# Holding two weight loads behind the stores of a pair's finer sums in a planned MoE kernel

## The chip, the cores and the metric

The kernel runs on one core of one Trainium2 chip. The metric is the device time of one execution in microseconds, as the median of the runs shown. One further execution was recorded by the hardware profiler; every view of the profile quoted here comes from such an execution. TensorE is called PE, its weight load PEld, VectorE DVE, ScalarE ACT, GpSimd POOL. SP is the engine whose queue carries most DMAs.

## The reference

A linear attention over 8 batches and 8 heads (576 tokens, head size 64) gives x with 4608 rows and 512 columns. Then comes a mixture of 8 experts in which every row goes through every expert:

```python
logits = x @ w_gate
P = np.exp(logits - logits.max())
for _ in range(8):                      # the routing
    P /= P.sum(1, keepdims=True) + 1e-09
    P /= P.sum(0, keepdims=True) + 1e-09
    P *= N / E
for e in range(E):
    h = np.maximum(x @ w1[e], 0.0)      # up:   512 -> 1024
    out += P[:, e:e + 1] * (h @ w2[e])  # down: 1024 -> 512
```

## The kernel before

**Stages.** The attention of all batches takes the first 203 us of the profiled execution. In its gaps, expert 0 already runs for the groups of 512 rows whose x is complete (`up0`, L1005, and `down0`, L1010). Next, expert 0's remaining groups fill PE while DVE does the eight rounds of the routing (`routing`, L1146). In each round DVE makes column sums `cs` (L1170, split into three bf16 parts at L1179), one small PE matmul adds them over the partitions (`ps<-cs,colw` in the views, recorded under the helper's line L622), and DVE goes on from its result (L1185 to L1167 of the next round). Then experts 1 to 7 follow, about 107 us each. They use sums and differences of blocks (a fast matrix multiplication with seven products in place of eight), so the inputs x, the weights w1 and w2 and the hidden rows all need preparing subtractions on DVE (`sub`, L1236, whose instruction is recorded as L1240).

**The sums of x.** For each pair of row groups, `sums_x` (L1428) makes three combinations in buffers of the ring X and stores them to DRAM (L1422). For experts 2 to 7, three of the blocks get a second, finer level: `fine_x` (L1365) stores two parts of the block itself (L1369, L1371), makes four finer differences in one more buffer of X, and stores that buffer (L1385) to a DRAM tile Xi, one for each pair and block. The blocks are named "11", "21" and "t1", in this order. The ring X has four buffers (L492). Three are held by the pair's own sums while expert 1 works on that pair, so the three finer sums of a pair share the fourth: the subtractions of the next block wait until the store of the one before has landed. Pair 0's sums are made at 203 us, beside the routing; the other pairs' sums are made during expert 1. From expert 2 on, `load_fine` (L1389) reads everything back.

**The weights.** `load_w` (L514) loads both matrices of one expert, 2 MB of float32 in DRAM each, which become bf16 on the way, by two DMAs from POOL (L517). w1 and w2 have two buffers each, one of them a view of a tile `wx` that the attention uses before (tile `w` is the other). `sums_up` (L1242) and `sums_down` (L1291) prepare them; the second writes its results into `hx`. From expert 1 on, POOL's other work is the additions into acc (L1875) and some of M (L1643).

**What sets the order.** Nothing is written to an engine directly. Every operation is registered in a plan (`Plan.op`) with keys that it reads (r) and writes (w), and a duration. `Plan.schedule` (L271) then plays the whole program through and always starts the operation with the earliest possible time, ties by registration (L302). What results is one fixed list. `Plan.run` (L337) goes through that list and emits the instructions, so that each engine gets its own in that order and runs them strictly in that order; the waits between engines are made by the framework from the tiles that an instruction really reads and writes. The keys themselves are no waits on the chip. Only one rule is carried over as a wait of its own, for operations of DVE and POOL at a port that they share (`behind`).

**How the plan reckons DMAs.** `dma` (L428) gives every transfer a time on a link: bytes over a speed (L425; 540 bytes per ns for the sums' stores, 400 for the weights, L433). `Links` (L127) has one line for POOL's transfers and one for all others, each in order. A transfer joins its line 3.1 us after the issue on POOL and 1.6 us after it elsewhere (L136); it lands 1.0 us after its link time (L307). While both lines are busy, each is slowed:

```python
share = [1.0, 1.0]
if len(on) == 2:
    a, b = (x[0][2] for x in self.line)
    all_ = (0.61 if a.turn else 0.84) / (a.unit + b.unit)
    share = [all_ * a.unit, all_ * b.unit]
```

A store of the sums has unit 50, a weight matrix 150, so a store then goes at 0.84 * 50 / 200 = 0.21 of its speed and the load at 0.63.

**The loop over experts**, around the change (L1978 on): for each expert `load_w` is registered first; for expert 1 with the key "late" (the attention's buffers are free), for later ones also with a key of acc that expert e-1 writes, which places the loads late in that expert. Then expert 1 registers `sums_x` of pair 0; `sums_up`, `sums_down` and the loop over the pairs follow.

Of the kernel before, what the change touches and what calls it, by code (L numbers as in the profile page):

```python
# [349 lines left out]
def kernel(  # L350
# [44 lines left out]
    acc = [accp.tile([128, 4, DD], FP32, name=f"acc{g}", tag=f"acc{g}") for g in range(NA)]  # L395
# [12 lines left out]
    late = {}  # L408
# [19 lines left out]
    def dma(queue, nbytes, rate, fn, r=(), w=()):  # L428

        speed, unit = LINK.get(rate, (rate, 40))  # L430
        if nbytes == 2 << 20:
            speed, unit = 400, 150
        o = plan.op(queue, 0.8 if queue == "POOL" else 0.6, 0.0, fn, r, w, (), nbytes / speed)  # L433
        o.turn, o.unit = rate == 148, unit
# [71 lines left out]
    def new(tag):  # L506
        return R[tag].new()
# [3 lines left out]
        return buf().bitcast(BF16)  # L511


    def load_w(e, r=()):  # L514
        w1, w2 = new("w1"), new("w2")
        for w, src in ((w1, moe_w1), (w2, moe_w2)):
            dma("POOL", 2 << 20, 280, lambda w=w, src=src: nc.gpsimd.dma_start(  # L517
                out=w(), in_=src[e].rearrange("(c p) f -> p c f", p=128)),
                r, [(w, i, j) for i in range(2) for j in range(2)])
        return w1, w2  # L520
# [510 lines left out]
    for b in range(2):  # L1031
# [4 lines left out]
        w=["wphi_f0"])  # L1036
    dma("ACT", 1 << 15, 100, lambda: nc.scalar.dma_start(out=wphi_f[64:128, :], in_=w_phi),
        w=["wphi_f1"])
# [13 lines left out]
    for i in range(2):  # L1052
        dve(450, lambda i=i: nc.vector.memset(vrd[i], 0.0),
            w=[("vrd", i, h, *y) for h in range(2) for y in ((), (1,))])
# [181 lines left out]
    def sub(eng, el, out_, x, y, op, r, w):  # L1236
        f = nc.vector if eng is dve else nc.gpsimd
        kw = {"shared": True} if eng is dve else {}
        eng(el * 0.5 if eng is dve else el * 1.04 + 128,
            lambda: f.tensor_tensor(out=out_(), in0=x(), in1=y(), op=op), r, w, **kw)  # L1240

    def sums_up(e, w1):  # L1242

        def q(i, j):
            return lambda: w1()[:, 2 * j:2 * j + 2, 512 * i:512 * i + 512]

        S = [None] + [new("T") for _ in range(3)]

        def s(n):
            return lambda: S[n]().rearrange("p (a b) -> p a b", a=2)  # L1250


        a11, a12, a21, a22 = (1, 0), (1, 1), (0, 0), (0, 1)
        late = ["late"] + (["P"] if e == 1 else [])

        def k(a):
            return [(w1, *a)]

        sub(dve, 1024, s(2), q(*a11), q(*a21), ALU.subtract, k(a11) + k(a21) + late, [S[2]])
        sub(dve, 1024, q(*a21), q(*a21), q(*a22), ALU.add, k(a22) + late, k(a21))  # L1260
        sub(dve, 1024, s(1), q(*a21), q(*a11), ALU.subtract, k(a21) + k(a11) + late, [S[1]])
        sub(dve, 1024, s(3), q(*a12), s(1), ALU.subtract, k(a12) + [S[1]] + late, [S[3]])
        A = {"11": (q(*a11), k(a11)), "12": (q(*a12), k(a12)), "22": (q(*a22), k(a22)),
             "s1": (q(*a21), k(a21)), "s2": (s(1), [S[1]]), "s3": (s(2), [S[2]]),
             "s4": (s(3), [S[3]])}
        if e > 1:
            for n in INNER:
                fine_up(A, n)
        return A

    def fine_up(A, n):

        f, r = A[n]
        t, key, first = FINE_W[n]

        def a(q, k):
            return lambda: f()[:, k, :].rearrange("p (f q c) -> p q f c", f=2, q=2)[:, q]

        def s(n):
            return lambda: t()[:, n]  # L1280

        def step(n, x, y, op, r, w):
            sub(dve, 256, s(n), x, y, op, r, [(key, n), *w])

        step(0, a(1, 0), a(1, 1), ALU.add, r, first)
        step(2, a(0, 0), a(1, 0), ALU.subtract, r, [])
        step(1, s(0), a(0, 0), ALU.subtract, [*r, (key, 0)], [])
        step(3, a(0, 1), s(1), ALU.subtract, [*r, (key, 1)], [])
        A[n + "*"] = t, [(key, i) for i in range(4)]
# [28 lines left out]
    def xq(gs, i, j):  # L1318

        n = len(gs)  # L1320
        return lambda: xT[:, 2 * i:2 * i + 2, 512 * gs[0]:512 * (gs[0] + n)].rearrange(
            "p k (a b) -> p a k b", a=n)[:, :, :, 256 * j:256 * j + 256]

    def xall(gs):
        return [k for g in gs for k in xkeys(g)]
# [12 lines left out]
    class Turns:  # L1338
# [4 lines left out]
        def next(self):  # L1343
# [16 lines left out]
    Xi = {(g[0], n): dram.tile([128, 7, 256], BF16, name=f"xi{g[0]}{n}")  # L1360
          for g in pairs for n in INNER.values()}
# [54 lines left out]
    def new_x():  # L1416
        return {n: new("X") for n in (2, 3, 4)}

    def move_x(gs, n, store, X):
        d, t = (lambda: Xd[gs[0], n][:, 0:len(gs)]), (lambda: X[n]()[:, 0:len(gs)])  # L1420
        if store:
            dma("SP", len(gs) << 17, 160, lambda: nc.sync.dma_start(out=d(), in_=t()),  # L1422
                [X[n]], [("Xd", gs[0], n)])
        else:
            dma("SP", len(gs) << 17, 160, lambda: nc.sync.dma_start(out=t(), in_=d()),
                [("Xd", gs[0], n)], [X[n], "order of X"])

    def sums_x(gs, r0=()):  # L1428

        X = new_x()  # L1430

        def x(n):
            return lambda: X[n]()[:, 0:len(gs)]

        b11, b12, b21, b22 = (xq(gs, *ij) for ij in ((0, 1), (0, 0), (1, 1), (1, 0)))
        el, keys = 512 * len(gs), xall(gs)
        r = keys + ["late", *r0]
        sub(dve, el, x(3), b22, b12, ALU.subtract, r, [X[3], "order of X"])
        sub(dve, el, b12, b12, b11, ALU.subtract, ["late", *r0], keys)
        sub(dve, el, x(2), b22, b12, ALU.subtract, r, [X[2]])  # L1440
        sub(dve, el, x(4), b21, x(2), ALU.subtract, r + [X[2]], [X[4], "order of X"])
        for n in (3, 2, 4):
            move_x(gs, n, True, X)
        if len(gs) == 2:
            for n, b in (("22", b22), ("11", b11), ("21", b21), ("t1", b12)):
                if n in INNER.values():
                    fine_x(gs, n, b, r0)
                else:
                    for a in range(2):
                        dma("SP", 1 << 17, 160, lambda n=n, a=a, b=b: nc.sync.dma_start(  # L1450
                            out=Xp[gs[0], n][:, a], in_=b()[:, a]), r, [("Xp", gs[0], n, a)])
        return X
# [507 lines left out]
    def take():  # L1960
        z = [new(f"H{n}") for n in sorted(slots[:2])]
        del slots[:2]
        return z
# [13 lines left out]

    early, dn = [plain(8)], plain(7)  # L1978
    for e in range(1, E):
        w1, w2 = load_w(e, ["late", ("acc", 4, 0, 0)] if e > 1 else ["late"])  # L1980
        if e == 1:
            nextX = sums_x(pairs[0])
        A7 = sums_up(e, w1)
        B7 = sums_down(e, w2) if e > 1 else None
        turn = [*pairs, (8,)] if e < E - 1 else [(8,), *pairs]
        if e == 2:
            o = plan.op("X", 0.0, 0.0, lambda: None, w=["K"])
            for d in plan.ops[:-1]:
                if any(b.ring is R["X"] for b in d.bufs):
                    d.users.append(o)  # L1990
                    o.deps.append(d)
                    o.left += 1
        for n, gs in enumerate(turn):
            if (e, n) == (1, 4):
                plan.inorder = 1
            X = nextX if e == 1 else load_fine(gs)
            H = {g: [] for g in gs}
            for fp in range(len(gs)):
                hs = take()
                for i, z in enumerate(hs):  # L2000
                    H[gs[min(i, len(gs) - 1)]].append(z)
                fine = e > 1 and len(gs) == 2
                if fine:
                    un = up49(A7, fp, X, H, gs, ["up0", "K"])
                else:
                    un = up7(A7, gs, fp, X, H, ["up0"])
                for o in UNITS[turns.pop(0)]:
                    if o in un:
                        un[o]()
                    elif len(o) == 3:  # L2010
                        un[o[:2], int(o[2])]()
                    elif dn is not None:
                        dn[o]()
                if dn is not None:
                    dn["out"]()
                    slots.extend(dn["slots"])
                if e == 1 and fp == 0 and n + 1 < len(turn):
                    nextX = sums_x(turn[n + 1], [(H[gs[0]][0], 0, 1, 1)])
                if B7 is None and fp:
                    B7 = sums_down(e, w2)  # L2020
                if fp == len(gs) - 1:
                    wait += [(e, g, H[g], B7, w2, [z.ring.number for z in H[g]]) for g in gs]
                dn = next_down()
# [35 lines left out]
```

## Time and profile before

| what | value |
|---|---|
| median of 3 runs | 1010.11 us (1009.81 to 1011.59) |
| profiled execution, its time | 1010.62 us |
| its span from first to last instruction | 1008.8 us |
| PE, DVE, ACT, POOL busy | 994.0, 898.6, 812.8, 447.6 us |
| both loads of expert 1 issued at | 203.4 and 204.2 us |
| both loads of expert 2 issued at | 316.0 and 316.8 us |

How to read the views: times are microseconds from the start of the span. A row of the order of time gives start, duration, engine, line, operation, written tile <- read tiles, the count of merged instructions, and in brackets the engine's idle time before it with what ended it. A row of the waits gives who waited for whom, the total, the number of times, and the longest. A row of the chain of work gives start, length and what the end of the program then depended on. SPq is SP's queue, and its rows are issues of DMAs; "DMA to landing" is the time from an issue until its data have arrived. PE's matmul rows overlap in time (each is pipelined behind the one before), so their starts tell the rate. A row of the table by stretches gives the stretch, its length, and then the busy time of PE, PEld, DVE, ACT and POOL with counts.

### The profile page before, as it was taken

The page shows a single profiled execution, that of the slowest core. Times are in us where ns is not written, and L with a number is a line of the kernel's source. Part 1 is how long each engine was busy: PE and PEld are TensorE (multiplying, and loading weights), DVE is VectorE, ACT ScalarE, POOL GpSimd, SP SyncE. Part 2 cuts the span into 40 slices and gives each one's busy share as a digit, 9 for nine tenths or more (in the row PEclk, how much of TensorE's full clock was granted, in tenths as well). Part 3 has the DMA queues.
Part 4 walks back from the last instruction along what each step waited for, and adds up shares of the span by engine and source line. Part 5 has one row for each costly group of instructions (what it writes and reads, how often), then busy time and mean ns, then how long its engine had stood idle before and what let it go on. Part 6 is the DMA issues. An engine that isn't in the chain of part 4 may idle for free.

```text
span 1008.8 us, 23309 instructions
## 1 busy us (share of the span) xinstructions
PE 994.0 (99%) x8376; PEld 727.7 (72%) x8376; DVE 898.6 (89%) x1999; ACT 812.8 (81%) x1930; POOL 447.6 (44%) x514
## 2 busy tenths in 40 slices
PE   7899999999999999999999999999999999999998
PEld 5666666644566877777777877787778777787775
DVE  7999998987888998899989898989889988989886
ACT  7999999845979788878878788777887888778874
POOL 5778674400133344434444444444443444344443
PEclk9999999999999999999999999999999999999999
DMA  9999999181136423282327133632246222724653
GB/s 249 183 202 183 157 153 144 38 170 56 53 121 143 147 97 98 84 184 96 109 98 170 44 100 131 130 127 98 97 117 177 97 98 84 147 79 142 208 174 126
DMA packets 129748, 128.86 MB, mean 128 GB/s; under 512 B 55776, under 2 KB 98272, under 8 KB 129632
## 3 DMA queue, kind: packets, MB, share of 16 engines
q1 hardware_dynamic: 97680, 103.33, 36.3%
q0 software_dynamic: 31648, 23.86, 16.9%
q8 instruction: 65, 1.06, 0.5%
q14 instruction: 51, 0.42, 0.2%
q10 hardware_dynamic: 304, 0.20, 0.1%
HBM read 122.50 MB, written 19.53 MB: 141 GB/s over the span
## 4 chain that ended last, share of the span: by engine, by line
PE 92%; DVE 3%; ACT 2%; DMA 2%; issue 1%; POOL 0%; DVEq 0%
PE ps L1466 41%; PE ps L1475 20%; PE ps L622 17%; PE ps L1607 11%; PE ps L905 2%; DMA xi6t<-X 1%; DMA xi<-X 1%; PE ps L752 1%; ACT q L618 0%; DVE m L614 0%; ACT k L618 0%; DVE wx L614 0%; DVE X L1240 0%; DMA acc<-in_k_dram 0%; DVE hs L1676 0%
## 5 line engine op out<-in xcount | busy, mean ns | idle before, releaser
L1875 POOL TENSOR_TENSOR acc<-acc,hx 128x512 f32<-128x512 f32 x186 | 236.1, 1276 | 404.7 <-ACT hx L1872 135.0
L1466 PEld LDWEIGHTS <-hs 128*128 128x128 bf16 x1984 | 194.1, 98 | 46.4 <-issue 0.2
L1872 ACT ACTIVATE hx<-ps,P 128x256 f32<-128x256 f32 x372 | 158.9, 483 | 53.4 <-PE ps L1466 52.0
L1860 DVE SCALAR_TENSOR_TENSOR acc<-ps,P,acc 128x256 f32<-128x256 f32 x372 | 162.2, 478 | 30.2 <-PE ps L1466 28.2
L1475 PE MATMUL ps<-xT,T 128*128 128x512 bf16 x608 | 171.0, 379 | 0.0
L1466 PEld LDWEIGHTS <-hx 128*128 128x128 bf16 x1488 | 145.6, 98 | 24.9
L1466 PE MATMUL ps<-hx,hs 128*128 128x256 bf16 x992 | 144.3, 273 | 0.0
L1676 DVE CUSTOM_DVE_ANT_0 hs<-ps,U 128x512 bf16<-128x512 f32 x192 | 124.7, 684 | 11.3 <-PE ps L1475 6.6
L1607 PE MATMUL ps<-xT 128*128 128x256 bf16 x576 | 125.4, 272 | 0.0
L1475 PEld LDWEIGHTS <-T 128*128 128x128 bf16 x672 | 65.8, 98 | 40.6
L1682 ACT ACTIVATE hs<-ps 128x512 bf16<-128x512 f32 x96 | 55.9, 598 | 41.7 <-PE ps L1475 40.2
L1466 PE MATMUL ps<-wx,hs 128*128 128x256 bf16 x560 | 78.4, 273 | 0.0
L622 PE MATMUL ps<-w,hx 128*128 128x512 bf16 x288 | 73.0, 379 | 0.0
L622 PE MATMUL ps<-xT,w 128*128 128x512 bf16 x288 | 72.9, 379 | 0.0
L1466 PE MATMUL ps<-wx,hx 128*128 128x256 bf16 x496 | 72.3, 273 | 0.0
L1676 DVE CUSTOM_DVE_ANT_0 hs<-ps,X 128x512 bf16<-128x512 f32 x96 | 65.1, 684 | 7.8 <-PE ps L1607 6.9
L1466 PE MATMUL ps<-hx 128*128 128x256 bf16 x496 | 71.2, 273 | 0.0
L1607 PEld LDWEIGHTS <-xT 128*128 128x128 bf16 x576 | 56.3, 98 | 17.5
L1466 PE MATMUL ps<-w,hx 128*128 128x256 bf16 x432 | 62.2, 273 | 0.0
L614 DVE TENSOR_REDUCE m<-ps 128x4 f32<-128x512 f32 x88 | 58.8, 680 | 3.7 <-PE ps L622 1.9
L1672 ACT COPY X<-ps 128x512 f32<-128x512 f32 x96 | 58.6, 610 | 2.5 <-DVE ps L1650 2.5
L1466 PE MATMUL ps<-w,hs 128*128 128x256 bf16 x432 | 60.2, 273 | 0.0
(174 smaller groups left out, 2256.0 us busy)
## 6 DMA issues: line engine op xcount, KB each, us to landing
xT<-xi SPq DMA_DIRECT2D x48, 448.0 KB, 4.6
xT<-xd SPq DMA_DIRECT2D x72, 256.0 KB, 4.0
wx<-in_moe_w_dram POOLq DMA_DIRECT2D x8, 1024.0 KB, 11.2
v_m<-in_v_dram SPq DMA_DIRECT2D x15, 512.0 KB, 5.2
out_dram<-acc SPq DMA_DIRECT2D x14, 512.0 KB, 3.0
w<-in_moe_w_dram POOLq DMA_DIRECT2D x6, 1024.0 KB, 11.0
xT<-xp SPq DMA_DIRECT2D x24, 256.0 KB, 2.8
qk<-in_k_dram POOLq DMA_DIRECT2D x12, 256.0 KB, 5.4
```

The costliest lines, as they stand in the source:

```text
L614: dve(el, lambda: nc.vector.tensor_reduce(out=dst(), in_=src(), axis=AX.X, op=ALU.max, apply_absolute_value=True), r, w)
L622: nc.tensor.matmul(out_, lhsT=lhsT, rhs=rhs, start=start, stop=stop)
L905: pe(65, lambda j=j: nc.tensor.matmul(pn()[:, j * D1:j * D1 + D1], lhsT=s["T"][x]()[:, j % 2, 2 * h + j // 2, :] if j < 4 else r["T"][x]() ...
L1466: pe(256, lambda i=i, k=k, z=z: nc.tensor.matmul(bank()[:, 256 * i:256 * i + 256], lhsT=lhs(k, i), rhs=rhs(k), start=first and z, stop=k = ...
L1475: pe(512, lambda k=k: nc.tensor.matmul(bank().rearrange("p (a b) -> p a b", a=2), lhsT=lhs(k), rhs=rhs(k), start=first and k == 0, stop=k ...
L1607: pe(256, lambda: nc.tensor.matmul(halves_of(bank[q], n)(), lhsT=lhs(), rhs=t()[:, rhs, :], start=start, stop=True, skip_group_check=True) ...
L1672: act(512, lambda: nc.scalar.copy(out=flat(to[q])(), in_=bank[q]()), [bank[q]], [(to[q], 0), (to[q], 1)])
L1676: dve(515, lambda: nc.vector._custom_dve(ADD_SAT, out=out_(q, i, j), in0=bank[q]().rearrange("p (a b) -> p a b", a=2), in1=to[q](), s0=3.0 ...
L1682: act(512, lambda: nc.scalar.activation(out=out_(q, i, j), in_=bank[q]().rearrange("p (a b) -> p a b", a=2), func=ACT.Relu, bias=0.0, scal ...
L1860: dve(320, lambda n=n, ts=ts: nc.vector.scalar_tensor_tensor(out=acc[g][:, ts, 256 * j:256 * j + 256], in0=bank()[:, 256 * n:256 * n + 256 ...
L1872: act(370, lambda n=n: nc.scalar.activation(out=u()[:, n, :], in_=bank()[:, 256 * n:256 * n + 256], func=ACT.Copy, bias=0.0, scale=P[:, 4 ...
L1875: pool(695, lambda: nc.gpsimd.tensor_tensor(out=acc[g][:, 2 * i:2 * i + 2, 256 * j:256 * j + 256], in0=acc[g][:, 2 * i:2 * i + 2, 256 * j: ...
```

## The change

`load_w` takes one set of keys for w1 (`r`) and another for w2 (`r2`). For experts 1 and 2, w2's set gets one more key: the last store (part 2, the finer differences) of block "t1" of pair 0 for expert 1, and of pair 6 (row groups 6 and 7) for expert 2. The key must exist when the load is registered, so expert 1's `sums_x` of pair 0 is registered ahead of its loads. Experts 3 to 7 keep their keys.

```diff
-    def load_w(e, r=()):
+    def load_w(e, r, r2):
         w1, w2 = new("w1"), new("w2")
-        for w, src in ((w1, moe_w1), (w2, moe_w2)):
+        for w, src, r in ((w1, moe_w1, r), (w2, moe_w2, r2)):
             dma("POOL", 2 << 20, 280, lambda w=w, src=src: nc.gpsimd.dma_start(
                 out=w(), in_=src[e].rearrange("(c p) f -> p c f", p=128)),
                 r, [(w, i, j) for i in range(2) for j in range(2)])
...
     for e in range(1, E):
-        w1, w2 = load_w(e, ["late", ("acc", 4, 0, 0)] if e > 1 else ["late"])
         if e == 1:
             nextX = sums_x(pairs[0])
+        r = ["late", ("acc", 4, 0, 0)] if e > 1 else ["late"]
+        stored = [("Xi", 6 * (e - 1), "t1", 2)] if e < 3 else []
+        w1, w2 = load_w(e, r, r + stored)
         A7 = sums_up(e, w1)
```

## The prediction

> **What bounds the kernel now.** I read the page's span and busy shares first, then the chain of work that ended last, then the waits of PE, then the order of time on POOL, DVE and PE around the two loads that the diff touches.
>
> ```profile
> span 1008.8 us, 23309 instructions
> PE 994.0 (99%) x8376; PEld 727.7 (72%) x8376; DVE 898.6 (89%) x1999; ACT 812.8 (81%) x1930; POOL 447.6 (44%) x514
> PE 92%; DVE 3%; ACT 2%; DMA 2%; issue 1%; POOL 0%; DVEq 0%
> 336.00:960.00 624.00, 623.85 (x5007) 489.67 (x5006) 563.36 (x1212) 499.75 (x1215) 274.44 (x260) 1.00 0.41 116
> ```
>
> The reader is to see that TensorE is the limit: 994.0 of 1008.8 us busy, 92% of the chain. The last row is one long stretch, experts 2 to 7: PE is busy 623.85 of its 624.00 us, so a change can give back almost nothing there (0.15 us), but a stop of PE anywhere is paid in full. From 200 us on, the view of waits names two stops of PE, and the order of time has them with their places:
>
> ```profile
> PE ps L1475 <- DVE hs L1530: 0.6, 1, 0.6
> PE ps L622 <- DVE cs L1179: 0.4, 1, 0.4
> 228.10 0.19 PE L622 MATMUL ps<-cs,colw 128*128 128x24 bf16 x1 [0.36 <-DVE cs L1179]
> 330.20 1.19 PE L1475 MATMUL ps<-X,wx 128*128 128x512 bf16 x4 [0.62 <-DVE hs L1530]
> 223.50 0.49 DVE L1240 TENSOR_TENSOR X<-xT 128x256 bf16<-128x256 bf16 x2 [1.49 <-DMA xi<-X]
> ```
>
> The second row belongs to the routing: the cs matmul comes late because DVE stood 1.49 us before it, at a subtraction into X, until a store of X had landed. So a store's landing is on the path now, at expert 1. What hangs there is 0.4 us of PE, at expert 2 0.6 us: about 1.0 us (0.1%) is all that an earlier landing can earn.
>
> **Step 1, what the edit does on the chip at expert 1: nothing by itself.** The new keys are read by the planner alone (Plan.op); run (L337) issues the operations in the planner's order, and the chip waits only for data, buffers and the one rule that run adds. A load of w2 neither reads nor writes Xi. So the edit acts through places in the queues only, and POOL's are these:
>
> ```profile
> 203.41 1.74 POOL L517 DMA_DIRECT2D wx<-in_moe_w_dram  x2 [7.21 <-PE ps L622]
> 269.95 1.27 POOL L1875 TENSOR_TENSOR acc<-acc,hx 128x512 f32<-128x512 f32 x1 [64.80 <-ACT hx L1872]
> DMA to landing us min/median/max: 10.4/13.8/17.2
> ```
>
> The two loads of expert 1 stand next to each other (0.83 and 0.90 us make the 1.74), and POOL's next instruction comes 65 us later. Wherever in that gap the planner now puts w2, it remains POOL's next instruction behind w1 and is issued at 204.2 as before. It lands 17.2 us later, at 221.4; its traffic beside the stores stays. Nothing is queued behind it for 64.8 us. The Trainium skill, DMA: Bandwidth & Descriptors, section "Two DMAs through the same engine are not ordered", says that a DMA is held behind another only when its issuing engine waits on the other's completion semaphore, and that a place in a queue is no substitute. By that rule there is no hold here; if the edit did make such a semaphore, the sum would be that of the first rival.
>
> **Step 2, what it does to the planned order: DVE's place moves.** The planner expects the stores earlier, since it thinks that w2 is held. Its own figures (L425 to L433, L136, L149) serve here only to find a place in the order; every duration charged comes from the trace.
>
> ```profile
> 204.54 0.35 SPq L1422 DMA_DIRECT2D xd<-X  x1
> 217.08 0.32 SPq L1385 DMA_DIRECT2D xi<-X  x1
> SPq L1371 <- DMA xd<-X: 2.4, 2, 1.4
> 217.08 6.40 DMA xi<-X
> 216.69 0.67 DVE L1170 TENSOR_REDUCE cs<-T 128x8 f32<-128x288 f32 x1
> 217.40 0.37 DVE L1179 TENSOR_TENSOR cs<-cs 128x8 f32<-128x8 f32 x2
> 221.65 0.37 DVE L1179 TENSOR_TENSOR cs<-cs 128x8 f32<-128x8 f32 x2
> 218.03 0.18 PE L622 MATMUL ps<-cs,colw 128*128 128x24 bf16 x1
> ```
>
> The store that frees X (L1385) stands eleventh on SP behind the first at 204.54. To the planner these eleven are 3.3 us of link work (four of 0.49, four of 0.24, three of 0.12), a load 5.2 us. While both lines are busy, stores go at 0.21 of their speed and the load at 0.63. Before: two loads, 10.5/0.63 = 16.6 us, cover all the stores, 3.3/0.21 = 15.6 us; with 1.6 us of lead-in and 1.0 of landing from 204.5 that is about 222. The trace agrees: the waiting subtractions (223.50) were put right behind the two L1179 of 221.65, which end at 222.0. After: only w1 is beside them, 5.2/0.63 = 8.3 us, in which 1.75 us of stores pass; the other 1.5 us go unshared. That is 8.3 + 1.5 = 9.8 instead of 15.6 us, and the planned landing moves from 222 to 216.2, or to 217.2 if w1 comes on the link later than the first store. I take 217.2: the four subtractions then stand between L1170 and L1179 of an earlier round of the routing, at about 217.3.
>
> **Step 3, the stop.** The real landing does not move: it was 217.08 + 6.40 = 223.48, with the DMAs ahead slow beside both loads (the SP row above is a store held by the landing of an older, unrelated one). So DVE stands at the subtractions from 217.3 to 223.5, 6.2 us, and cs, which PE needs for its matmul planned near 218.0, stands behind them. Today L1179 ends at 217.77 and the matmul starts at 218.03: a slack of 0.26. PE stops 6.2 - 0.26 = 5.9 us; the 0.36 of 228.10 is then gone, so **+5.5**. Ends: behind the two L1179 (217.8) the next cs is hit instead, 0.9 less, +4.6; a slot earlier, before L1170 (216.7), +6.2. No other work can cover it, since PE runs its list in order. The second store (224.64 now) is issued behind these subtractions as today, so a second stop is not charged.
>
> **Step 4, the slow start after a stop.** No stop of this length stands in the middle of this trace. The one comparable row is the start, where PE had idled 3.99 us:
>
> ```profile
> 3.99 1.99 PE L752 MATMUL ps<-identf,acc 128*128 128x128 f32 x8 [3.99 <-DMA acc<-in_k_dram]
> 9.86 1.04 PE L622 MATMUL ps<-wphi,qkT 128*128 128x256 bf16 x8
> 14.71 2.03 PE L752 MATMUL ps<-identf,acc 128*128 128x128 f32 x16 [0.29 <-ACT kr L618]
> ```
>
> Eight transposes took there what sixteen take at 14.71, and full speed is back by 9.86: 5.8 us at half speed, 2.9 us lost. Behind a stop of 5.9 us I bound this by 0 and 2.9 and take **+2.0**, nearer to the only row. The Trainium skill, TensorE: Matmul & The Clock Gate, Part 1, says that an idle window of about 3.4 us halves the clock until a busy window has passed; an estimate from that page is half of 3.4 to 6.8, so 1.7 to 3.4 us, and the trace's 2.9 agrees with it; by the page alone 0 would not be an end.
>
> **Step 5, expert 2.** Here POOL has other work in the gap, so the load of w2 does move:
>
> ```profile
> 316.00 1.69 POOL L517 DMA_DIRECT2D w<-in_moe_w_dram  x2
> 319.68 2.63 POOL L1875 TENSOR_TENSOR acc<-acc,hx 128x512 f32<-128x512 f32 x2 [1.98 <-DVE hx L1240]
> 335.69 3.83 POOL L1875 TENSOR_TENSOR acc<-acc,hx 128x512 f32<-128x512 f32 x2 [13.38 <-DVE hx L1240]
> DMA to landing us min/median/max: 9.5/11.9/14.3
> 317.00 7.75 DMA xi6t<-X
> 324.77 0.42 DVE L1240 TENSOR_TENSOR X<-xT 128x512 bf16<-128x512 bf16 x1 [1.01 <-DMA xi6t<-X]
> 365.24 0.69 DVE L1240 TENSOR_TENSOR hx<-w 128x1024 bf16<-128x1024 bf16 x1
> ```
>
> To the planner the store, issued 1.0 us behind w1, lands before w1 is on the link (1.0 + 1.6 + 0.5 + 1.0 = 4.1 us after w1's issue), near 320.1, so w2 goes behind one or both of the additions of 319.68: issue at 321 to 322.3 instead of 316.8, about 5 us later. The store is out at 317.00 and lands at 324.75, before w1 lands (316.0 + 9.5 = 325.5): the loads pass one behind the other, so it is w1 that slows the store, and w1 stays. I charge **0**; the ends are -0.6 (the whole stop of 330.20) and 0. The later landing (at most 331.1 + 5.5 = 336.6) is covered by 28 us until w2 is first read at 365.24. An addition that now waits 0.9 us behind the load is covered by the 13.38 us that POOL idles next. Of what the new order does elsewhere I know nothing; bounds -0.2 (PE's 0.15 of idle) and +0.6 (the longest stop that a misplaced operation has now), taken as 0.
>
> **Sum:** 5.5 + 2.0 + 0 + 0 = 7.5 us. Ends: 4.6 + 0 - 0.6 - 0.2 = 3.8 and 6.2 + 2.9 + 0 + 0.6 = 9.7. The profiled execution took 1010.62 (span 1008.8 and 1.8 around it) and would take 1018.1; the median of the runs shown is 0.5 lower, so **1017.6**, with 1013.9 to 1019.8.
>
> **Rivals.** (a) *The hold is real* (the other side): w2 of expert 1 leaves only once the stores have landed. Then they run beside w1 alone; the 1.49 us of DVE and with them 0.36 of PE go, at most 0.62 at expert 2 as well: -1.0 us, 1009.1. It decides from the point where the actual landing comes before the new place of the subtractions, 217.3. Against it: POOL's row, with no instruction between the loads. For it: only the diff's words. Chance 0.08. (b) *The order hardly moves*: DVE's subtractions stay behind 221.65 because something else holds them in the plan; same stops, 1010.1. For it: the old place agrees with my sum only to half a microsecond; against it: the sum moves by over 4.8. Chance 0.17. (c) *A short stop*: the place moves by half as much, to about 219.5; DVE stops 4.0, PE 4.0 - 0.26 - 0.36 = 3.4 more than now, too short for a slow start: 1013.5. Chance 0.15. The forecast with its ends has 0.60.
>
> **How the numbers follow.** Both signs are possible, but what can be gained is 1.0 us while the stop is several. The range 1009.8 to 1019.8 takes in the forecast, (b) and (c); outside are (a) and a loss above 9.7, about 0.15. About 0.2% (2 us) is what a measurement of this kernel tells from no change: faster by that 0.03 (the bound of (a) lies within, so this is a new order that saves more than I can see), within 0.27 (most of (a), (b) and some of (c)), slower 0.70.
>
> **What would show it.** Right: POOL's two L517 of expert 1 still together near 203.4; a wait of DVE at L1240 for xi<-X of 5 to 7 us near 217 to 223; PE waiting 5 to 6 us for cs L1179, then some 5 us of matmuls at twice their spacing; w2 of expert 2 near 322; all of 336 to 960 as before, only later. Wrong: w2 of expert 1 issued after 220; the subtractions still behind the fourth cs; or a PE stop at another line.

## The result, and the profile after

The changed kernel takes 1017.64 us (median of 6 runs, 1016.93 to 1018.7), the kernel before 1010.38 (6 runs): a ratio of 1.0072, 95% interval 1.0059 to 1.0085, or 7.26 us more. The profiled execution took 1017.61 us with a span of 1015.8, so 7.0 more than the span before.

The page of the changed kernel, and its table by stretches. The columns are the stretch, its length, busy time of PE, PEld, DVE, ACT and POOL with counts, then the granted clock of PE, the share of DMA, and GB/s:

```profile
span 1015.8 us, 23274 instructions
PE 993.1 (98%) x8340; PEld 728.3 (72%) x8376; DVE 898.4 (88%) x1999; ACT 813.4 (80%) x1930; POOL 448.3 (44%) x514
```

```profile
203.00:245.00 42.00, 35.59 (x189) 16.23 (x192) 29.46 (x86) 15.30 (x27) 1.73 (x2) 0.92 0.50 109
343.00:967.00 624.00, 623.85 (x5009) 489.69 (x5007) 563.41 (x1213) 500.27 (x1215) 274.90 (x260) 1.00 0.41 117
```

The same stretch in the kernel before:

```profile
203.00:245.00 42.00, 41.64 (x229) 19.14 (x228) 35.95 (x102) 16.50 (x30) 1.74 (x2) 1.00 0.51 109
```

PE's busy time is nearly the same in both kernels; what grew is the span. Experts 2 to 7, 336 to 960 before and 343 to 967 after, have the same 623.85 us of busy PE in 624.00, only 7.0 us later. The loss is therefore made ahead of 343, and nearly all of it in the 42 us of the routing: PE is busy 6.05 us less there, and its clock is 0.92 where it was 1.00. The waits of PE between 200 and 343 us and the order of time on DVE and PE give the place:

```profile
PE ps L622 <- DVE cs L1179: 6.2, 1, 6.2
PE ps L1475 <- DVE hs L1530: 0.7, 1, 0.7
```

```profile
215.87 0.46 DVE L1167 TENSOR_TENSOR T<-L,rr 128x288 f32<-128x288 f32 x1
222.98 0.29 DVE L1240 TENSOR_TENSOR X<-xT 128x256 bf16<-128x256 bf16 x1 [6.65 <-DMA xi<-X]
223.19 0.66 DVE L1170 TENSOR_REDUCE cs<-T 128x8 f32<-128x288 f32 x1
```

```profile
217.48 0.81 PE L622 MATMUL ps<-xT,w 128*128 128x512 bf16 x3
224.46 0.20 PE L622 MATMUL ps<-cs,colw 128*128 128x24 bf16 x1 [6.17 <-DVE cs L1179]
224.51 2.29 PE L622 MATMUL ps<-xT,w 128*128 128x512 bf16 x5
226.59 2.52 PE L622 MATMUL ps<-w,hx 128*128 128x512 bf16 x8
228.95 1.67 PE L622 MATMUL ps<-xT,w 128*128 128x512 bf16 x7
```

The reader is to see one chain. DVE reaches a subtraction into X at 216.3 and stands 6.65 us until the store of the block before has landed; L1170, which makes cs and needs nothing of that store, is queued behind it; PE stands 6.17 us for cs. In the kernel before, the same subtractions came at 223.50, behind two more cs. The store itself is where it was, by the chain of work:

```profile
216.55 6.41 DMA xi<-X
```

It took 6.40 us before. The store itself is only half of the delay: its data were ready at 209.35, where DVE's last subtraction of that block ends, and SP issued it 7.2 us later, because SP's queue stood for the landings of older stores (the view of its waits names xd and xp). The two weight loads did not part at expert 1, and at expert 2 the second one left 4.6 us behind the first (POOL's order of time):

```profile
203.09 1.73 POOL L517 DMA_DIRECT2D wx<-in_moe_w_dram  x2 [7.21 <-PE ps L622]
276.95 1.27 POOL L1875 TENSOR_TENSOR acc<-acc,hx 128x512 f32<-128x512 f32 x1 [72.13 <-ACT hx L1872]
323.00 0.79 POOL L517 DMA_DIRECT2D w<-in_moe_w_dram  x1
326.39 1.26 POOL L1875 TENSOR_TENSOR acc<-acc,hx 128x512 f32<-128x512 f32 x1 [2.59 <-DVE hx L1240]
327.61 0.93 POOL L517 DMA_DIRECT2D w<-in_moe_w_dram  x1
```

The first row is again two issues next to each other, with nothing behind them for 72 us. The hold that the change speaks of does not exist at expert 1.

After PE's restart the clock shows in the table by stretches of 2 us:

```profile
220.00:222.00 2.00, 0.00 (x0) 0.00 (x0) 0.00 (x0) 0.00 (x0) 0.00 (x0) 0.76 1.09 369
222.00:224.00 2.00, 0.00 (x0) 0.00 (x0) 1.02 (x4) 0.00 (x0) 0.00 (x0) 0.50 0.12 39
226.00:228.00 2.00, 2.00 (x6) 0.70 (x5) 1.89 (x4) 0.60 (x1) 0.00 (x0) 0.54 0.35 131
228.00:230.00 2.00, 2.00 (x11) 0.88 (x9) 0.94 (x5) 0.60 (x1) 0.00 (x0) 1.00 0.00 0
```

The clock falls to 0.50 while PE stands and is back at 1.00 by 228. Thirteen matmuls start within 4.44 us (224.51 to 228.95) that need 2.80 at full speed (the same rows of phys_after below, 217.60 to 220.40).

**The account** of the profiled execution: stop at cs 6.17 instead of 0.36, +5.8; slow start 4.44 - 2.80 = +1.6; expert 2's stop 0.69 instead of 0.62, +0.1; the attention ended 0.3 earlier in this execution (DVE's first subtraction at 203.32, before at 203.64), -0.3. That makes 7.2, and the spans differ by 7.0. The end of the attention moves like this from one profiled execution to the next (DVE's first subtraction comes between 202.6 and 204.0 us in those below), and the ends of matmuls are modelled, so such a sum is good to about 0.5 us.

### The profile page after: what moved, and what is told of

Same layout as the page of the kernel before. It is cut to its first block, busy times and chain, and to the rows that moved or that the text cites. A ratio compares the mean times of both kernels' runs of the same rounds, so it can differ in the third digit from the quotient of the medians.

```text
span 1015.8 us, 23274 instructions
## 1 busy us (share of the span) xinstructions
PE 993.1 (98%) x8340; PEld 728.3 (72%) x8376; DVE 898.4 (88%) x1999; ACT 813.4 (80%) x1930; POOL 448.3 (44%) x514
## 4 chain that ended last, share of the span: by engine, by line
PE 91%; DVE 3%; DMA 3%; ACT 3%; issue 1%; SPq 0%; DVEq 0%
PE ps L1466 41%; PE ps L1475 20%; PE ps L622 16%; PE ps L1607 11%; PE ps L905 2%; DMA xp<-xT 1%; ACT q L618 1%; DMA xi6t<-X 1%; ACT k L618 1%; DMA xi<-X 1%; PE ps L752 0%; DVE m L614 0%; DVE X L1240 0%; DVE wx L614 0%; DMA acc<-in_k_dram 0%
## 5 line engine op out<-in xcount | busy, mean ns | idle before, releaser
L1475 PE MATMUL ps<-xT,T 128*128 128x512 bf16 x608 | 171.1, 379 | 0.0
L1607 PE MATMUL ps<-xT 128*128 128x256 bf16 x576 | 125.4, 272 | 0.0
L1475 PEld LDWEIGHTS <-T 128*128 128x128 bf16 x672 | 65.7, 98 | 40.7 <-issue 0.2
L622 PE MATMUL ps<-w,hx 128*128 128x512 bf16 x275 | 70.6, 381 | 0.5
L1607 PEld LDWEIGHTS <-xT 128*128 128x128 bf16 x576 | 56.3, 98 | 17.5
L983 ACT ACTIVATE hx<-ps 128x512 bf16<-128x512 f32 x72 | 43.5, 659 | 22.5 <-PE ps L622 22.3
```

What stands on the lines that cost most here:

```text
L622: nc.tensor.matmul(out_, lhsT=lhsT, rhs=rhs, start=start, stop=stop)
L983: act(512 * n, lambda f0=f0, ph=ph, ht=ht: nc.scalar.activation(out=ht()[:, f0 % 4:f0 % 4 + n, :].rearrange("p a b -> p (a b)"), in_=ph()[ ...
L1475: pe(512, lambda k=k: nc.tensor.matmul(bank().rearrange("p (a b) -> p a b", a=2), lhsT=lhs(k), rhs=rhs(k), start=first and k == 0, stop=k ...
L1607: pe(256, lambda: nc.tensor.matmul(halves_of(bank[q], n)(), lhsT=lhs(), rhs=t()[:, rhs, :], start=start, stop=True, skip_group_check=True) ...
```

## The experiments

The theory: the new key is a wait in the plan only; the planner, believing the load held, expects the store of X sooner and places DVE's subtractions ahead of L1170, where they stand for a store that lands as late as ever. Rivals: the later load at expert 2 costs the time; the new order costs time by itself; the hold is real and something it moves is late. Each ratio is to runs of the kernel before on the same chip; their median was 1010.38 us in the first batch, 1010.30 in the second and 1010.15 in the third.

### One expert at a time

```diff
-        stored = [("Xi", 6 * (e - 1), "t1", 2)] if e < 3 else []
+        stored = [("Xi", 6 * (e - 1), "t1", 2)] if e == 1 else []      # e1_only
+        stored = [("Xi", 6 * (e - 1), "t1", 2)] if e == 2 else []      # e2_only
```

> Only expert 1 gets the new key; expert 2's loads are as before. My theory (the planned place of DVE's subtractions at expert 1 causes the whole loss): +7.2 us, 1017.6, with DVE's wait of 6.65 us for xi<-X, PE's stop of 6.2 us before the cs matmul and the slow matmuls behind it all there. Rival (the later second load of expert 2 causes a part): the loss is smaller by that part, below 1017.

> Only expert 2 gets the new key; its second load goes behind one addition on POOL and leaves about 4 us later. My theory: 0, 1010.4 within 0.5 us, PE's stop of 0.6 us near 330 unchanged, because the first load is what slows the store. Rival (the store lands sooner when the second load stays away): -0.6 us, 1009.8. Rival (the later load costs): above 1011.

e1_only took 1018.71 us (ratio 1.0078, 1.0063 to 1.0094), e2_only 1010.55 (0.9999, 0.999 to 1.0008). So the whole loss hangs on the key of expert 1, and the key of expert 2 is worth nothing measurable. PE in e1_only, at the routing:

```profile
224.95 0.20 PE L622 MATMUL ps<-cs,colw 128*128 128x24 bf16 x1 [6.01 <-DVE cs L1179]
225.00 2.29 PE L622 MATMUL ps<-xT,w 128*128 128x512 bf16 x5
227.08 3.57 PE L622 MATMUL ps<-w,hx 128*128 128x512 bf16 x8
230.49 1.68 PE L622 MATMUL ps<-xT,w 128*128 128x512 bf16 x7
```

The stop is that of the changed kernel. The slow matmuls behind it last longer (thirteen take 5.49 us, 225.00 to 230.49, and not 4.44), which is where this kernel's 1.1 us above the changed one come from. In e2_only the load does move, POOL's order of time and the chain of work show, but the store in front of it lands no sooner:

```profile
315.14 0.80 POOL L517 DMA_DIRECT2D w<-in_moe_w_dram  x1
318.54 1.26 POOL L1875 TENSOR_TENSOR acc<-acc,hx 128x512 f32<-128x512 f32 x1 [2.60 <-DVE hx L1240]
319.76 0.92 POOL L517 DMA_DIRECT2D w<-in_moe_w_dram  x1
```

```profile
316.15 7.70 DMA xi6t<-X
```

That is 7.70 us, with the second load issued 3.6 us behind the store, against 7.75 before with both loads issued ahead of it. To move the second load changes nothing for this store.

### The planner's belief without the edit, and the edit with a real hold

lie_small is the kernel before with no new key; the planner alone is told that w2 of expert 1 has 1 KB, while the real transfer keeps its size. hold_e1 has the key for expert 1 and, on the chip, a wait of w2's issue for the last finer store.

```diff
# lie_small, on the kernel before: n is what the planner is told
-    def load_w(e, r=()):
+    def load_w(e, r=(), size=2 << 20):
...
-        for w, src in ((w1, moe_w1), (w2, moe_w2)):
-            dma("POOL", 2 << 20, 280, lambda w=w, src=src: nc.gpsimd.dma_start(
+        for w, src, n in ((w1, moe_w1, 2 << 20), (w2, moe_w2, size)):
+            dma("POOL", n, 280, lambda w=w, src=src: nc.gpsimd.dma_start(
...
+                        1 << 10 if e == 1 else 2 << 20)      # the size, where load_w is called
# hold_e1, on the changed kernel with the key at expert 1 alone: ins is the issue of w2
...
+            tc.add_manual_dep(
+                ins.ins, put[6 * (e - 1), "t1"].ins.ins.name, mybir.DependencyInfo(
+                    mybir.DependencyClass.Sync, mybir.DependencyReason.DATA),
+                reason="the stores first")
```

One more thing goes with the lie: the planner knows a weight matrix by its 2 MB, so any other size also gets its general speed and unit (380 and 60, and not 400 and 150).

> The kernel before, with no new key and the same registration; the planner alone is told that the second load of expert 1 has 1 KB instead of 2 MB (the transfer on the chip is the same). The two loads keep their places; DVE's list at expert 1 becomes that of the changed kernel. My theory: the place alone makes the loss, so 1017.6 as in the changed kernel. Rival (the held load, the key or the registration matters): 1010.4.

> The key for expert 1 alone, and now a real wait on the chip as well: the second load's issue waits on the completion of the last finer store. My theory: the place of DVE's subtractions is that of the changed kernel, but the store now really lands early, about 6 us before 223 (one load's transfer less ahead of it, some 6.2 us), near 217; DVE stops 1 us, PE under 1 us, no slow matmuls: 1010.0 to 1011.2. Rival (to hold the load is what costs, or its traffic later): 1015 to 1018 as without the real wait.

lie_small took 1018.89 us (1.0086, 1.0072 to 1.0099). Without any key it has the order of DVE that the changed kernel has at the routing, and the same stop:

```profile
223.70 0.29 DVE L1240 TENSOR_TENSOR X<-xT 128x256 bf16<-128x256 bf16 x1 [6.64 <-DMA xi<-X]
```

hold_e1 took 1010.16 us (1.0001, 0.9992 to 1.0009). Its subtractions have the same early place (lines are 11 higher in this kernel), and now the store is really early. POOL, the chain of work, DVE and PE:

```profile
226.51 0.88 POOL L528 DMA_DIRECT2D wx<-in_moe_w_dram  x1 [22.23 <-DMA xi0t<-X]
```

```profile
214.27 3.20 DMA xi<-X
```

```profile
217.50 0.29 DVE L1251 TENSOR_TENSOR X<-xT 128x256 bf16<-128x256 bf16 x1 [0.81 <-DMA xi<-X]
```

```profile
218.98 0.19 PE L633 MATMUL ps<-cs,colw 128*128 128x24 bf16 x1 [0.33 <-DVE cs L1190]
```

So the belief alone makes the loss, and making the belief true takes it away. A true hold is worth no more than that: the store is issued 2.3 us sooner than in the changed kernel (214.27 and 216.55) and takes 3.2 us less, so it lands 5.5 us sooner; but the subtractions were placed sooner as well, and PE still stands 0.33 us where it stood 0.36 before.

### How the cost goes with the place: two more lies

The same edit with 1 MB (lie_1m) and 384 KB (lie_384) in place of 1 KB. The planner then puts the subtractions into later slots, so that a shorter stop is left.

> As the kernel before, but the planner takes the second load of expert 1 for 1 MB instead of 2 MB (the transfer on the chip is the same). DVE's subtractions then stand behind L1161 of the fourth round, at about 219.5 on the clock of the kernel before. My theory: DVE stops 223.5 - 219.5 = 4.0 us, PE 3.7, so +3.3 us without a slow start (1013.7) and up to 1.7 us more with one (1015.4). Rival (the loss does not follow the place): 1010.4 or 1017.6.

> The same with 384 KB: the subtractions stand behind L1185 of the fourth round, at about 218.8. My theory: DVE stops 4.7 us, PE 4.4, +4.0 us without a slow start (1014.4), up to 1.7 us more with one (1016.1). Together with the run before it shows from which stop on PE restarts slowly.

lie_1m took 1013.47 us (1.0029, 1.0018 to 1.0041), 0.2 below the lower end that was expected, and not by the sum that gave it: PE's stop is 3.14 us and not 3.7, and there is a slow start. PE's order of time and clock:

```profile
225.23 0.17 PE L622 MATMUL ps<-cs,colw 128*128 128x24 bf16 x1 [3.14 <-DVE cs L1179]
225.25 2.60 PE L622 MATMUL ps<-w,hx 128*128 128x512 bf16 x8
227.65 2.91 PE L622 MATMUL ps<-xT,w 128*128 128x512 bf16 x8
230.39 1.67 PE L622 MATMUL ps<-w,hx 128*128 128x512 bf16 x7
```

```profile
224.00:226.00 2.00, 0.77 (x5) 0.41 (x5) 1.60 (x7) 0.00 (x0) 0.00 (x0) 1.00 0.35 131
226.00:228.00 2.00, 2.00 (x7) 0.71 (x5) 1.29 (x4) 0.00 (x0) 0.00 (x0) 0.57 0.00 0
```

A stop of 3.14 us is enough for a slow start: sixteen matmuls take 5.14 us (225.25 to 230.39) where sixteen take 3.44 at full speed (two eights of 1.72), 1.7 lost. The clock here falls only some 1 us after PE has started again. With the stop that is 3.14 - 0.36 + 1.7 = 4.5 in the profiled execution, whose span grew by 3.0; its attention ended 1.1 us earlier than that of the kernel before, and the other 0.4 lie within the accuracy of the sum. The median grew by 3.2; whether the attention ends early in all of this kernel's executions, one profile cannot tell.

lie_384 took 1024.89 us (1.0154, 1.0137 to 1.0171), a miss by about 9 us. The stop at cs is there but shorter than expected (DVE 4.32 us and not 4.7, PE 3.57 and not 4.4). The planner also wrote a different order for experts 1 and 2, and that lost more than the stop. PE at the routing, and the first expert's length behind 343 us:

```profile
226.06 0.18 PE L622 MATMUL ps<-cs,colw 128*128 128x24 bf16 x1 [3.57 <-DVE cs L1179]
```

```profile
343.00:450.00 107.00, 102.09 (x795) 77.39 (x794) 91.63 (x201) 81.55 (x201) 45.73 (x44) 1.00 0.30 91
```

The kernel before has 107.00 of 107.00 us busy in a stretch of this length from 336. The missing 4.9 us are in the main ten stops of PE between 356 and 374 us, 0.2 to 1.0 us each, for results of ACT and DVE; none is for a DMA. This run says nothing against the theory of the stop, but it says that an edit to one transfer in the plan can cost 5 us in a place that has nothing to do with it.

### Other buffers, first by the plan and then behind its back

If the stop comes only from the shared fourth buffer of X, then buffers of their own for pair 0's finer sums must remove it while w2 stays unheld. own_after gives them slots of hs (the tile of the hidden rows, free until 254 us) in the changed kernel. own_w1 does the same without the key at expert 1 and with it on both loads of expert 2.

```diff
+    OWN = {"11": "H5", "21": "H4", "t1": "H3"}      # names of slots of hs
...
-        y = new("X")
+        y = new(OWN[n] if gs[0] == 0 else "X")
```

> The changed kernel, but the three finer sums of pair 0 get a buffer each, in hidden-row tiles that are free until expert 1 works, instead of taking turns in the one buffer of X. No subtraction has a store to wait for, wherever it is placed. My theory: no stop of DVE for xi<-X, no slow matmuls, 1009.6 to 1010.6. Rival (the held load costs by itself): 1017.6.

> The kernel before with the same own buffers for pair 0, and at expert 2 both loads, the first too, get the key of the store (planner only). The first load leaves some 4 us later, behind the addition near 320, so the store of 317 should land in 2 to 4 us and not in 7.75. Theory: both stops of PE that DMAs cause (0.4 and 0.6 us) go, 1009.4. Rival (the first matrix is then late for its sums): above 1011.

own_after took 1021.91 us (1.011, 1.0095 to 1.0125), own_w1 1019.15 (1.0092, 1.0077 to 1.0107): both missed in the total. The table by stretches of own_after has the stop gone and something else in its place:

```profile
203.00:245.00 42.00, 42.00 (x232) 19.55 (x230) 35.49 (x102) 16.66 (x30) 1.74 (x2) 1.00 0.50 109
343.00:450.00 107.00, 102.10 (x792) 76.98 (x790) 93.49 (x205) 81.15 (x200) 43.77 (x42) 1.00 0.29 80
```

The routing is perfect, 42.00 of 42.00 us at a clock of 1.00, and expert 2 is 4.9 us short, as in lie_384. In own_w1 the same two stretches have 42.00 and 101.07. The plan knows of the buffers, so it had made a new order again, and the total compares two orders instead of one wait. In own_after the stops of PE early in expert 2 are the same ten as in lie_384. Why these orders leave PE short there was not followed up.

Late in expert 1 both also have a longer stop of PE where the kernel before has 0.62 us. These are the rows of own_after and of lie_384:

```profile
331.10 0.65 PE L1483 MATMUL ps<-X,wx 128*128 128x512 bf16 x2 [2.17 <-DVE hs L1538]
335.63 0.59 PE L1475 MATMUL ps<-X,wx 128*128 128x512 bf16 x2 [2.24 <-DVE hs L1530]
```

Behind the first the granted clock goes to half, 0.50 in 332 to 334. Behind the second it stays at 1.00.

Below its total, own_w1 did what was expected of it: both loads of expert 2 are issued behind pair 6's last finer store (324.87 and 322.20), that store lands within 2.3 us, and neither of the two stops of PE is left. The new order lost more than that.

So the next pair keeps the plan as it is (`y = new("X")` stays, and with it every place in every queue) and changes only where the data lie when the instruction is emitted. phys_after is the changed kernel with pair 0's finer sums in hs. The subtractions and the store then use own() in place of y(). phys_before is the kernel before with that and, for the 0.6 us stop at expert 2, pair 6's "t1" sums in columns of xT that are dead by then.

```diff
         y = new("X")
+        own = lambda: (late["hs"][:, 5 - [*INNER.values()].index(n), 0].rearrange(
+            "p q (k c) -> p (q k) c", k=2) if g == 0 else
+            xT[:, 0, 0:1024].rearrange("p (n c) -> p n c", n=4)   # phys_before alone
+            if (g, n) == (6, "t1") else y().rearrange("p a k c -> p (a k) c"))
```

> The changed kernel with its written order kept instruction for instruction; only the physical place of the first pair's finer sums of x differs: they lie in the three last slots of hs, which nothing writes before 254 us, so the subtractions of block 21 and t1 do not wait for an earlier store to land. Leaves out no work. Theory (the place of the subtractions in the written order costs time only through the wait on the store in their buffer): no wait of DVE on a store near 217 us, no stop of PE behind cs, clock 1.00 there, the rest as in the changed kernel with its 1 us wait at expert 2: 1009.8 to 1010.6. Rival (the order in itself, or the later load at expert 2, costs time): over 1013, up to 1017.6.

> The kernel before with its written order kept; the first pair's finer sums lie in the three last slots of hs as in the other kernel, and the last pair's t1 sums of expert 1 lie in columns of xT that are dead by then, so that neither the 0.4 us wait of PE near 217 us nor the 0.6 us wait near 330 us has a store behind it. Leaves out no work. Theory: both stops gone and nothing else moved, 1009.0 to 1009.8, 0.5 to 1.2 below the kernel before. Rival (the stops are covered by the PE work that follows, or something else is late in their place): within 0.2 of the kernel before.

phys_after took 1009.0 us (0.9988, 0.9979 to 0.9997), 0.8 below the range that was expected. With every instruction in the place that the changed kernel gives it, and w2 of expert 2 still late, it is 8.6 us faster than the changed kernel (ratios to the kernel before: 0.9988 and 1.0072). DVE, PE and the stretch:

```profile
215.31 0.46 DVE L1167 TENSOR_TENSOR T<-L,rr 128x288 f32<-128x288 f32 x1
215.69 0.28 DVE L1240 TENSOR_TENSOR hs<-xT 128x256 bf16<-128x256 bf16 x1
215.89 0.66 DVE L1170 TENSOR_REDUCE cs<-T 128x8 f32<-128x288 f32 x1
```

```profile
217.57 0.18 PE L622 MATMUL ps<-cs,colw 128*128 128x24 bf16 x1
217.60 1.24 PE L622 MATMUL ps<-xT,w 128*128 128x512 bf16 x5
218.68 1.89 PE L622 MATMUL ps<-w,hx 128*128 128x512 bf16 x8
220.40 1.67 PE L622 MATMUL ps<-xT,w 128*128 128x512 bf16 x7
```

```profile
203.00:245.00 42.00, 41.75 (x214) 19.31 (x216) 36.36 (x100) 17.21 (x32) 1.26 (x2) 1.00 0.50 110
```

These are the rows of the changed kernel without the 6.65 and the 6.17 us, and thirteen matmuls in 2.80 us. The rivals "the order by itself" and "the later load at expert 2" fall: both are in this kernel and cost nothing.

phys_before took 1007.96 us (0.9977, 0.9968 to 0.9986) and is the fastest kernel here, 2.2 us below the one before and 9.7 below the changed one. It was expected to gain 0.5 to 1.2, so the theory priced it too low. Both stops are gone, which is 1.0, and the view of PE's waits is empty between 200 and 343 us:

```profile
316.00:343.00 27.00, 27.00 (x204) 19.74 (x203) 24.62 (x61) 23.03 (x49) 9.50 (x7) 1.00 0.86 210
```

The attention ended 0.4 us earlier in the profiled execution. Counted from there, PE's first matmul of expert 1 (L1475) comes 0.67 us sooner than in the kernel before, and its first of expert 2 (L1607) 1.45 us sooner, so the two places give back more than the 0.36 and 0.62 us that their stops are given. No view names the rest, and it stays open.

## Why the prediction came out right, point by point

The forecast was 1017.6 us, by +7.5; measured were 1017.64 and +7.26.

- **Step 1, no hold at expert 1: right.** POOL's two issues are together at 203.09. hold_e1, in which the wait exists, shows what the row would have looked like: POOL stands 22.23 us, and the second issue comes at 226.51.
- **Step 2, the place of the subtractions: right in kind, one slot off.** They stand ahead of L1170, the end that was given as "a slot earlier", and not between L1170 and L1179. Of the two planned landings that it gave, 216.2 fits this place and 217.2, which it took, does not (its terms as written, 204.5 + 1.6 + 9.8 + 1.0, make 216.9). lie_small shows that the planner's reckoning of the transfers moves them: no key, same place, same loss.
- **Step 3, the stop: right.** 6.17 - 0.36 = 5.8 us against +5.5, within 4.6 to 6.2. The one slot earlier should have made it 6.2. The store landed 0.5 us sooner than assumed, 0.2 when counted from the end of the attention; and one assumption was wrong without hurting: PE's matmul for cs did not keep its place. Twenty matmuls stand between it and the cs matmul ahead of it, where the kernel before has eighteen, and the two more (0.43 us) cover a part of the wait. The removal of this wait at an unchanged order, phys_after, is worth 8.6 us: the stop (6.2), the slow start (1.6), and 0.8 that no row names. No second stop came, as assumed.
- **Step 4, the slow start: right in kind, and its size in part luck.** It is 1.6 us against +2.0. With the same stop it is larger elsewhere: thirteen matmuls take 4.84 us in lie_small (225.23 to 230.07) and 5.49 in e1_only, so 2.0 and 2.7 are lost. The three kernels differ in when the clock falls. By stretches of 1 us it is at half for 6.8 us in each, from 221.0 in the changed kernel, 222.6 in lie_small and 223.6 in e1_only; PE restarts at 224.46, 225.18 and 224.95, so that 3.4, 4.2 and 5.5 us of slow clock are left for its work, and half of that is lost. No row of the kernel before says when the clock will fall. An estimate by the figures of the Trainium skill, TensorE: Matmul & The Clock Gate, Part 1, was 1.7 to 3.4 us. The runs with a stop of some 6 us have 1.6 to 2.7. The idle window of about 3.4 us that the prediction takes from that page of the skill is not the least stop that matters here: 2.17 us (own_after) and 3.14 us (lie_1m) were enough.
- **Step 5, expert 2: right.** The second load moved by 3.8 us, where about 5 were forecast (e2_only: 319.76 and 315.14, where before the two stood next to each other) behind one addition, the store kept its 7.7 us, and e2_only is worth 0.9999. The addition that now follows the load cost nothing.
- **Elsewhere: right for this change, and luck in part.** Whatever the new order moved in experts 2 to 7, that stretch kept its 623.85 us of busy PE. But lie_384 and own_after lost 5 us there by edits no larger than this one. The bound of -0.2 to +0.6 was read from stops that an order already has; a new order can make new ones, and no view of the kernel before bounds that.
- **The rivals.** (a) was priced at -1.0 us, for both experts. With a real hold at expert 1 alone (hold_e1) the ratio is 1.0001, so nothing is gained, because a plan that believes in the early store also uses it, and the same small stop comes back at the earlier place. (b) and (c) did not occur; lie_1m is in effect (c), at 1013.47 against the 1013.5 given, but not by its sum: that took a stop of 3.4 us more than before as too short for a slow start, and lie_1m has one behind 3.14 us.
- **The total: luck in its last digits.** The forecast missed by 0.04 us because errors cancel: stop +0.3, slow start -0.4, expert 2 +0.1, and a kernel before that was measured 0.27 us slower beside the changed one than in the runs the forecast starts from. e1_only and lie_small, with the same place and the same stop, are 1.1 and 1.3 us slower.

## What to carry to other kernels

Where a planner writes the order and the hardware only keeps the order of each queue, a key that is no wait on the chip changes what the planner believes, not what happens; ask where each consumer is moved to by the belief, and what then stands behind it in its queue. A subtraction that waits for a buffer cost little here (0.36 us of PE) until an instruction that feeds the critical engine was queued behind it (6.17 us): give the buffer away before moving transfers, and test it at an unchanged order, since a new plan moves everything else too.

## What the runs showed of the hardware

- The length of a stop of PE alone does not say whether the granted clock falls: it went to half at a stop of 2.17 us (own_after) and one of 3.14 us (lie_1m), and stayed at 1.00 at one of 2.24 us (lie_384, 335.63).
- The fall can come after the restart: 1.05 us after it in lie_1m (1.00 in 224 to 226, 0.57 in 226 to 228). In the changed kernel, with 6.17 us, it came while PE stood (0.76 in 220 to 222).
- By stretches of 1 us, the clock is at half for 6.8 us at the stops of 6.0 to 6.2 us (changed kernel, e1_only, lie_small), and for 3.4 us at those of 2.2 to 3.6 us (own_after, lie_1m, and lie_384 at the routing). The work lost is half of what part of this lies behind the restart: 1.6, 2.7 and 2.0 us in the first three, 1.7 in lie_1m.
- Twelve 256 KB stores of the finer sums take 2.0 us in the median in the kernel before. One took 3.20 us behind other stores when no weight load was under way (hold_e1; its load had landed by 203.44 + 10.1 = 213.5). One took 6.41 us in the changed kernel beside a single load: two were issued, at 203.09 and 203.93, and they land 10.2 and 17.0 us after their issue, so one of them had landed by 214.1 at the latest. One load is enough to slow such a store.
- At expert 2 such a store took 7.75 us with both loads issued ahead of it, 7.70 with the second issued 3.6 us behind it (e2_only), and at most 2.3 with both behind it (own_w1). There the first load does the harm, and holding back the second alone changes nothing.
